# A first pair of heads prepared by a way of its own, and a new order of instructions within each pair: attention and routed experts on one core

## The chip, the cores and the metric

The kernel runs on one core of a Trainium2 chip. The metric is the device time of one launch in microseconds (us); the time of a kernel is the median of its runs. Inputs and output are float32 in the device's memory; the host only lays the inputs out anew.

The core's engines each run their own list of instructions in order: the tensor engine (PE) multiplies matrices, the vector engine (DVE), the scalar engine (ACT) and GpSimd (POOL) work elementwise or reduce, and SyncE (SP) issues most transfers (DMA). Engines wait for one another by semaphores.

## The reference

Attention over 64 heads (8 batches of 8 heads) with 1152 keys and head width 64, where two neighbouring queries are averaged first (576 queries a head), then a layer of 8 experts, to which the 4608 tokens are assigned greedily by score, at most 576 to each:

```python
# attention
q_pool = q.reshape(B, H, S // 2, 2, D).mean(axis=3)
scores = (1 / np.sqrt(D)) * np.matmul(q_pool, k.transpose(0, 1, 3, 2))
scores = scores - np.max(scores, axis=-1, keepdims=True)
attn = np.exp(scores)
attn = attn / (np.sum(attn, axis=-1, keepdims=True) + 1e-09)
out = np.matmul(attn, v)          # B=8, H=8, S=1152, D=64
# experts, on x = out as 4608 tokens of 512
logits = x @ w_gate               # 512 x 8
...
for idx in np.argsort(-logits.flatten()):      # greedy, capacity 576
    tok, e = divmod(int(idx), 8)
    if assigned[tok] < 0 and counts[e] < 576:
        assigned[tok] = e; counts[e] += 1
for e in range(8):
    out[assigned == e] = np.maximum(x[assigned == e] @ w1[e], 0) @ w2[e]   # 512 x 1024 x 512
```

## The kernel before

**Two stages.** The attention works on 32 pairs of heads, numbered 0 to 31. Then follow the assignment of tokens and the eight experts. The change lies in the attention; the code of the second stage is the same in both kernels.

**Precision.** Every number that enters a matmul is held as two 16-bit parts, high and low, whose products are added in float32. So each pair's q, k and v are split: a high part (KH, QH, the high half of V) is a scaled copy on ACT; a low part (KL, QL, the low half of V) is what the copy lost, made on DVE by one instruction that scales, subtracts and rounds (`scalar_tensor_tensor`). The scales SC and EX follow from sums of absolute values, so that the 16 bits are used well.

**The main loop.** A pair has 18 steps, two heads times nine blocks of 128 keys. In each step the PE makes scores (`qk`, L617, four matmuls of 288 columns into one of two score banks sc), ACT takes the exponential into P (L620), POOL takes P minus its upper 16 bits into PM (L623 and L624; at the steps listed in `AT["pd"]` DVE does it), and the PE multiplies P and PM with V (`av`, L634, 45 small matmuls), six steps behind the scores. At the end of a head the sums are divided out (L651 to L655). Every two pairs the gate's logits are added up (L669 to L687) and the attention's rows are stored (L749).

**The preparation of a pair** runs during the pair before it. In order: loads of q, k and v into one buffer each (QD, KD, VD: L410 to L418); q's two neighbours added (QS, L466, DVE); sums of absolute values on ACT (L427, with the scrap output VJ) and a matmul that totals them over the partitions (L431, L432); scales from the bits of the totals (VE L441, SC, EX L452 and L456); the parts QH L468, QL L470, KH L483, KL L486, V L509 and L512; copies of the parts by DMA to the layout of the score matmuls (`spread`, L493, into KA, KB, QA, QB, two buffers each). Then the row maxima of the scores, subtracted in the exponent: a block-diagonal copy of q (BD, L475, zero but for two blocks of 64 x 64) lets one matmul make the scores of both heads for 64 queries each (L535 and L545, in two banks ma and mb), and DVE reduces them (MX, L538 and L547). Nine query blocks times 1152 keys make 18 matmuls of 512 columns and some of 128. The maxima of a pair are gathered (CM, L573), transposed on the PE (L589), scaled (AU, L590), and written by DMA as an additional row of QB (L593); so the score matmul itself subtracts them.

**Pair 0** has nothing before it to hide its preparation. There BD is copied by DVE, the maxima come in 27 pieces of 384 columns (L526) into all eight PSUM banks, of which DVE reduces 18 (L530) and ACT copies nine to MS (L533), which DVE then folds (L566 to L568); one CM, one transpose (L582), and QB by DVE (L584) with the help of a diagonal mask `ndiag`, nine rows beside the 64 of a head. Before that the PE is warmed up by 50 matmuls of ones (wu, L756) and, during pair 0's maxima, by 65 more (wv, L758).

**What sets the order.** All of this is first written down as items with their reads and writes (class `Order`). For the attention the class `Cycle` then puts them in one order, from which each engine's list follows: of all items whose inputs' writers are placed, the one with the smallest number comes next. The number is looked up under the item's tag and its count within the pair, from the table TAU (from pair 1 on) or TAU0 (pair 0), plus 25 for each pair. So all pairs from 1 on have nearly the same order within, and each table entry moves an item in every pair. The tables' numbers have no meaning beyond their order. `lock` marks items that use the port which DVE and POOL share; `Cycle` doesn't read it.

## Time and profile before

| what | before |
|---|---|
| median of 3 runs | 1360.26 us (1359.87 to 1360.43) |
| the profiled execution, its device time | 1367.31 us |
| the profiled execution, span of the profile | 1365.5 us |
| PE busy | 1254.2 us, 92% |
| PE weight loads busy | 1014.6 us, 74% |
| DVE busy | 1047.8 us, 77% |
| POOL busy | 896.5 us, 66% |
| ACT busy | 806.9 us, 59% |
| mean granted PE clock | 0.968 of full speed |

Busy shares are over the whole span, in which the attention takes about the first 840 us. The page cuts the span into 40 slices and prints for each the busy tenths of an engine and the granted clock of the PE:

```profile
PE   5688899999999999999999999898999999999996
DVE  6699989899998998999999975877768768722220
POOL 2368677878788787787878872346576557568531
PEclk6899999999999999999999998999999999999998
```

One digit stands for 34.1 us. In the first two slices the PE is half busy, and its clock is granted only in part; from there to about slice 25 (the attention) PE and DVE are both near nine tenths; in the experts the PE alone is full. The heaviest groups of the attention on the engine that shares DVE's port and on ACT are:

```profile
L624 POOL TENSOR_TENSOR PM<-P 128x576 f16<-128x576 f32 x502 | 607.8, 1237 | 217.9 <-ACT P L620 109.4
L620 ACT ACTIVATE P<-sc,EX 128x576 f32<-128x576 f32 x576 | 407.1, 739 | 119.0 <-PE sc L617 113.5
```

A row names line, engine, operation, output and inputs with shapes, and the count; then the busy time and the mean ns of one; then the idle time just before these instructions and what ended most of it.

### The profile page before, as it was taken

The numbers are of one execution on the slowest core, as the hardware profiler recorded it, in microseconds if no ns is written. First come the engines' busy times: TensorE is split into PE (matmuls) and PEld (weight loads), VectorE is DVE, ScalarE is ACT, GpSimd is POOL, SyncE is SP. The second block draws the span as 40 slices with busy tenths as digits, with TensorE's granted clock in tenths as the row PEclk, the third lists the DMA queues.
The fourth block names the chain that finished last, engine by engine and source line by source line (L and its number), as shares of the span: only waits on it lengthen the run. The fifth ranks groups of instructions, "written<-read, shape, count | busy, mean of one in ns | idle before, by whom it ended". The sixth has DMA issues, their size and how long they took to land.

```text
span 1365.5 us, 38368 instructions
## 1 busy us (share of the span) xinstructions
PE 1254.2 (92%) x15456; PEld 1014.6 (74%) x15456; DVE 1047.8 (77%) x2618; ACT 806.9 (59%) x1426; POOL 896.5 (66%) x824
## 2 busy tenths in 40 slices
PE   5688899999999999999999999898999999999996
...
DVE  6699989899998998999999975877768768722220
...
POOL 2368677878788787787878872346576557568531
PEclk6899999999999999999999998999999999999998
...
GB/s 160 97 131 169 86 150 155 138 144 168 130 143 153 154 143 142 152 145 147 171 131 137 137 70 19 105 55 193 159 70 200 101 128 150 183 117 154 97 12 35
DMA packets 123534, 175.20 MB, mean 128 GB/s; under 512 B 49500, under 2 KB 86364, under 8 KB 121180
## 3 DMA queue, kind: packets, MB, share of 16 engines
...
q14 instruction: 57, 0.47, 0.1%
...
## 4 chain that ended last, share of the span: by engine, by line
PE 59%; DVE 21%; DMA 9%; issue 5%; ACT 4%; SPq 1%; POOL 0%; another core or an unknown queue 0%; DVEq 0%; POOLq 0%; ACTq 0%
PE ph L1340 13%; PE av L634 13%; PE po L1370 12%; PE sc L617 10%; DMA QA<-QH 6%; DVE MX L538 6%; DVE V L512 4%; PE mb L535 3%; PE ma L535 2%; DVE QS L466 2%; ACT VJ L427 2%; DVE QL L470 1%; DMA W<-in_w_dram,widx 1%; ACT P L620 1%; PE rt L1018 1%
## 5 line engine op out<-in xcount | busy, mean ns | idle before, releaser
L624 POOL TENSOR_TENSOR PM<-P 128x576 f16<-128x576 f32 x502 | 607.8, 1237 | 217.9 <-ACT P L620 109.4
L620 ACT ACTIVATE P<-sc,EX 128x576 f32<-128x576 f32 x576 | 407.1, 739 | 119.0 <-PE sc L617 113.5
L634 PEld LDWEIGHTS <-P 128*128 128x128 bf16 x5760 | 297.7, 98 | 32.5 <-issue 4.1
L634 PE MATMUL av<-V,P 128*128 128x65 f16 (+1 forms) x5760 | 308.8, 192 | 0.0
L634 PE MATMUL av<-V,PM 128*128 128x65 f16 x2880 | 298.6, 194 | 0.8 <-POOL PM L624 0.8
L634 PEld LDWEIGHTS <-PM 128*128 128x128 f16 x2880 | 264.6, 97 | 1.1 <-POOL PM L624 0.9
L617 PE MATMUL sc<-QA,KA 128*128 128x288 f16 x1152 | 236.8, 287 | 10.2 <-DMA QA<-QH 8.9
L617 PE MATMUL sc<-QB,KB 65*128 65x288 f16 (+1 forms) x1152 | 237.8, 287 | 0.0
L538 DVE TENSOR_REDUCE MX<-ma 128x1 f32<-128x512 f32 x279 | 191.0, 685 | 24.4 <-PE ma L535 22.9
L538 DVE TENSOR_REDUCE MX<-mb 128x1 f32<-128x512 f32 x279 | 190.8, 684 | 11.0 <-PE mb L535 10.4
L617 PEld LDWEIGHTS <-KA 128*128 128x128 f16 x1152 | 102.4, 97 | 105.5 <-issue 51.8
L1370 PE MATMUL po<-W2H,HX 128*128 128x512 f32 x512 | 164.7, 397 | 0.0
L1340 PE MATMUL ph<-XL,W1H 128*128 128x320 f32 (+1 forms) x512 | 156.2, 305 | 1.8 <-DVE XL L1273 1.3
L1340 PE MATMUL ph<-XH,W1H 128*128 128x320 f32 (+1 forms) x512 | 155.8, 304 | 0.3 <-DVE XL L1239 0.3
L1340 PE MATMUL ph<-XH,W1L 128*128 128x320 f32 (+1 forms) x512 | 155.7, 304 | 0.0
L1345 ACT ACTIVATE HX<-ph 128x320 fp32r<-128x320 f32 (+1 forms) x128 | 52.5, 411 | 148.9 <-PE ph L1340 138.8
L535 PE MATMUL mb<-KH,BD 128*128 128x512 f16 x279 | 107.8, 386 | 34.8 <-DVE MX L538 28.7
L617 PEld LDWEIGHTS <-KB 65*128 65x128 f16 (+1 forms) x1152 | 113.3, 98 | 30.5
L1370 PE MATMUL po<-W2L,HX 128*128 128x512 f32 (+1 forms) x320 | 126.7, 396 | 0.0
L535 PE MATMUL ma<-KH,BD 128*128 128x512 f16 x279 | 106.8, 383 | 7.5 <-DMA BD<-QH 6.1
L1384 POOL DMA_INDIRECT out_dram<-OT,idx x40 | 39.6, 990 | 109.0 <-ACT OT L1375 85.0
L1370 PEld LDWEIGHTS po<-W2H,HX 128*128 128x128 f32 x512 | 94.9, 188 | 17.9
...
## 6 DMA issues: line engine op xcount, KB each, us to landing
...
QA<-QH SPq DMA_DIRECT2D x128, 72.0 KB
...
```

Of the source, the lines that this page charges most:

```text
L427: od.add(t + AT["bq"] * (c == 1) + AT["bv"] * (c == 2), "ACT", dur, lambda c=c, src=src: nc.scalar.activation(VJ[:, :src.shape[1]], src, A ...
L512: od.add(t + AT["vh"] + AT["vd"] * s, "DVE", 725, lock=1, fn=lambda s=s: nc.vector.scalar_tensor_tensor(V16[i][:, s, :, 0:D], VD[0][:, s], ...
L535: od.add(t, "PE", 214, lambda: nc.tensor.matmul(m, BD[i][:, j, :], KH[i][:, 512 * c:512 * c + 512], start=True, stop=True), r=bd + [("KH", ...
L538: od.add(t, "DVE", 597, lambda: nc.vector.tensor_reduce(MX[i][:, j, c:c + 1], m, axis=AX.X, op=OP.max), r=[mk], w=[("MX", i, j, c)], tag=" ...
L617: nc.tensor.matmul(c[:, t, :288], a[i][:rows, s, ks], b[i][:rows, s, 288 * t:288 * t + 288], start=first, stop=not first)
L620: od.add(g + 0.1, "ACT", 624, lambda: nc.scalar.activation(p.rearrange("p (t q) -> p t q", t=2), c[:, :, :288], AF.Exp, scale=EX[n % 3][:, ...
L624: od.add(g + 0.2, en, dur, lock=1, fn=lambda: eng.tensor_tensor(pm, p, hi, op=OP.subtract), r=[("P32", g % NP)], w=[("PM", g % NM)], tag="pm")
L634: nc.tensor.matmul(out, w[:, qs], v, start=kb == 0 and j == 0 and y == 0, stop=kb == NKB - 1 and y == 2, skip_group_check=True)
L1340: nc.tensor.matmul(p, a[:, d, fs], b[:, d, qs], start=z == 0, stop=z == 11)
L1345: nc.scalar.activation(HH[:, f, qs], p, AF.Relu)
L1370: nc.tensor.matmul(o[:n], a[:, z, q0:q0 + n], b[:, z], start=z == 0 and y == 0, stop=z == 7, skip_group_check=True)
L1384: st = nc.gpsimd.indirect_dma_start(out=out, out_offset=bass.IndirectOffsetOnAxis(ap=idx[i][:n, c:c + 1], axis=0), in_=OT[ob][:n], in_offs ...
```

## The change

**Pair 0 by a way of its own.** The maxima are made head by head, directly from the first 64 or last 64 rows of QH and KH, so that no block-diagonal copy is needed: two heads times five query blocks (four of 128, one of 64) times three pieces of 384 keys are 30 matmuls, each reduced by DVE into MX0. Head 0 uses all eight banks, head 1 only ma and mb, while the scores of head 0 run. Each head has its own CM, transpose and two writes into QB (rows 64 to 68: five rows for 73 - 64 = nine before). ACT's copies to MS and the folds are gone. The sum of |k| is taken in two halves (VM has a fourth column, and the total another matmul). The parts are made on other engines: QH on DVE by `tensor_scalar`; k, q and v are scaled in place on ACT behind their high parts, and POOL subtracts (KL, QL, V low).

**Warm-ups.** Instead of 50 and 65 matmuls of 128 columns there are 30 and 22 of 512 columns; all may begin at once, and where each stands is a matter of the tables.

**Order.** There are three tables (pair 0, pair 1, and all later ones), and nearly all their numbers are new. The lists of steps whose PM is made on DVE become [9] for [8, 10, 11, 14] in pair 0 (`pd0`), [4, 12] for [5, 12] in pairs 1 to 30 (`pd`), and eleven steps for ten in pair 31 (`pd1`). Assumed lateness of loads (`late`) is altered too; `Cycle` doesn't read it.

The core of the diff (numbers of the tables left out but for two entries):

```diff
         def at(i):
             zero, tag, num, base = self.key[items[i][1]]
-            l = (TAU0 if zero else TAU)[tag]
+            l = (TAU, TAU0, TAU1)[zero][tag]
             return l[min(num, len(l) - 1)] + PERIOD * base
...
-       "ld": [-147.52, -112.42, -203.92], "ldv": [-55.79], "me": [-20.33, -12.03, -9.26], "mm": [-28.73, -28.43,
+       "kl": [-181.49, -190.11], "ld": [-81.78, -145.94, -308.78], "ldv": [-98.51], "me": [-20.17, -11.42, -6.47],
...
-AT = {"load": -12.4, ...
-      6, "np": 10, "nm": 10, "stick": 1, "nx": 3, "wu": 50, "pd": [5, 12], "wv": 65, "pd0": [8, 10, 11, 14], "pd1":
-      [1, 2, 4, 5, 6, 8, 10, 13, 16, 17], "d1": 2.0, "cw1": 0.7}
+AT = {"load": -14.1, ...
+      6, "np": 10, "nm": 10, "stick": 1, "nx": 3, "wu": 30, "pd": [4, 12], "wv": 22, "pd0": [9], "pd1": [0, 2, 5, 7,
+      8, 9, 10, 14, 15, 16, 17], "d1": 2.0, "cw1": 0.7}
...
+    wide = const.tile([128, 512], BF, name="wide")
+    nc.vector.memset(wide, 1.0)
...
-    VM = several(2, [128, 3], F32, "VM")
+    VM = several(2, [128, 4], F32, "VM")
-    MS = const.tile([128, NB, 384], BF, name="MS")
+    MX0 = const.tile([128, 2, 5, 3], F32, name="MX0")
...
+        if n == 0 and not a:
+            for z in range(2):
+                od.add(t, "ACT", 680, lambda z=z: nc.scalar.activation(
+                    VJ[:, :M], KD[0][:, z * M:z * M + M], AF.Abs, accum_out=VM[i][:, 3 * z:3 * z + 1]), ..., tag="abk")
...
+        if n == 0:
+            od.add(t + 1, "DVE", 640, lambda: nc.vector.tensor_scalar(QH[i], QS[0], QC, None, op0=OP.mult), lock=1, ..., tag="qh")
+            halves = [slice(z * M, z * M + M) for z in range(2)]
+            for z, h in enumerate(halves):
+                od.add(t + 1, "ACT", 665, lambda h=h: nc.scalar.activation(KH[i][:, h], KD[0][:, h], AF.Copy, scale=KS), ..., tag="kh")
+            for z, h in enumerate(halves):
+                od.add(t + 2, "ACT", 665, lambda h=h: nc.scalar.activation(KD[0][:, h], KD[0][:, h], AF.Copy, scale=KS), ..., tag="kd")
+            od.add(t + 2, "ACT", 665, lambda: nc.scalar.activation(QS[0], QS[0], AF.Copy, scale=QC), ..., tag="kd")
+            for z, h in enumerate(halves):
+                od.add(t + 3, "POOL", 1105, lambda h=h: nc.gpsimd.tensor_tensor(KL[0][:, h], KD[0][:, h], KH[i][:, h], op=OP.subtract), ..., tag="kl")
+            od.add(t + 3, "POOL", 1105, lambda: nc.gpsimd.tensor_tensor(QL[0], QS[0], QH[i], op=OP.subtract), ..., tag="ql")
+            return
...
-            if n:
-                od.add(t + 1.1, "SP", 650, bd(nc.sync.dma_start), ..., late=3500, tag="bdd")
-            else:
-                od.add(t + 1.1, "DVE", 230, lock=1, fn=bd(nc.vector.tensor_copy), ..., tag="bd")
+            od.add(t + 1.1, "SP", 650, bd(nc.sync.dma_start), ..., late=3500, tag="bdd")
...
+            if n == 0:
+                od.add(t, "ACT", 665, lambda s=s: nc.scalar.activation(V16[i][:, s, :, D:2 * D], VD[0][:, s], AF.Copy, scale=VS), ..., tag="vh")
+                od.add(t + .5, "ACT", 665, lambda s=s: nc.scalar.activation(VD[0][:, s], VD[0][:, s], AF.Copy, scale=VS), ..., tag="vd")
+                od.add(t + 1, "POOL", 1105, lambda s=s: nc.gpsimd.tensor_tensor(
+                    V16[i][:, s, :, 0:D], VD[0][:, s], V16[i][:, s, :, D:2 * D], op=OP.subtract), ..., tag="vl")
+                continue
...
         if n == 0:
-            banks = [(ma, "ma"), (mb, "mb")] + ...
+            h, j = j // 5, j % 5
+            banks = [(ma, "ma"), (mb, "mb")]
+            if not h:
+                banks += ...
             m, mk = banks[z % len(banks)]
+            r, q = slice(64 * h, 64 * h + 64), 128 if j < 4 else 64
+            od.add(t, "PE", 163, lambda: nc.tensor.matmul(
+                m[:q, :384], QH[i][r, 128 * j:128 * j + q], KH[i][r, 384 * c:384 * c + 384], start=True, stop=True), ..., tag="mm" + "01"[h])
+            od.add(t, "DVE", 463, lambda: nc.vector.tensor_reduce(MX0[:q, h, j, c:c + 1], m[:q, :384], axis=AX.X, op=OP.max), ..., tag="mr" + "01"[h])
+            return
-            if c < 2:
-                od.add(t, "DVE", 463, lambda: nc.vector.tensor_reduce(MX[i][:, j, c:c + 1], m[:, :384], axis=AX.X, op=OP.max), ..., tag="mr")
-            else:
-                od.add(t, "ACT", 371, lambda: nc.scalar.copy(MS[:, j], m[:, :384]), r=[mk], w=[("MS", j)], tag="mc")
...
-    def fold(j, t):
...
+                def both(h=h):
+                    nc.vector.tensor_reduce(CM[h][:, 64:68], MX0[:, h, :4], axis=AX.X, op=OP.max)
+                    nc.vector.tensor_reduce(CM[h][:64, 68:69], MX0[:64, h, 4], axis=AX.X, op=OP.max)
...
-    for _ in range(AT["wu"]):
-        od.add(-70, "PE", 60, lambda: nc.tensor.matmul(mb[:, :128], ones, ones, start=True, stop=True), w=["mb"], tag="wu")
-    for _ in range(AT["wv"]):
-        od.add(-42, "PE", 54, lambda: nc.tensor.matmul(av[1][:, :128], ones, ones, start=True, stop=True),
-               r=[("CM", 0, 0)], w=["av1"], first=-1, tag="wv")
+    for x in ("wu", "wv"):
+        for _ in range(AT[x]):
+            od.add(-70, "PE", 213, lambda: nc.tensor.matmul(av[1], ones, wide, start=True, stop=True), w=["av1"], tag=x)
```

What this makes of the engines' lists shows at three places. In the rows a name with a number is one buffer of a tile; L numbers are lines of the kernel they belong to.

**PE, at the end of the maxima that come ahead of the first score matmul (sc).** Before, pair 0's last maximum matmul and the transpose of its maxima, pair 1's totals of absolute values (down, floor, VM) and seven maxima matmuls of pair 1 (L535, of which the first is shown) stand ahead of the first scores:

```order
L526 MATMUL mb<-KH_83,BD_97 128x384
L582 MATMUL mb<-ident,CM_102 73x128
L431 LDWEIGHTS down
L431 MATMUL mb<-floor,down 128x4
L432 LDWEIGHTS down
L432 MATMUL mb<-VM_120,down 128x3
L535 LDWEIGHTS BD_98
L535 MATMUL ma<-KH_84,BD_98 128x512
```

After, the last of head 0's maxima matmuls, the transpose, and one matmul of head 1's maxima stand there:

```order
L564 LDWEIGHTS QH_88
L564 MATMUL av_158<-KH_85,QH_88 128x384
L618 MATMUL mb<-ident,CM_104 69x128
L564 LDWEIGHTS QH_88
L564 MATMUL mb<-KH_85,QH_88 128x384
L656 LDWEIGHTS KA_91
L656 MATMUL sc_155<-QA_95,KA_91 128x288
```

So the first scores (L656, L617 before) come behind the maxima of one head of pair 0 rather than behind those of both heads and a part of pair 1's.

**DVE, in a pair of the steady stretch.** Before, from the first piece of V's low part on (MX are maxima; ma and mb the banks; QS the sum of two neighbouring queries):

```order
L512 SCALAR_TENSOR_TENSOR V_99<-VD_117,SC_109,V_99 128x9x64
L538 TENSOR_REDUCE MX_125<-mb 128x1
L538 TENSOR_REDUCE MX_125<-ma 128x1
L470 SCALAR_TENSOR_TENSOR QL_88<-QS_118,SC_109,QH_86 128x576
L512 SCALAR_TENSOR_TENSOR V_99<-VD_117,SC_109,V_99 128x9x64
L466 TENSOR_TENSOR QS_118<-QD_116 128x576
L538 TENSOR_REDUCE MX_125<-mb 128x1
```

After, in the same place:

```order
L550 SCALAR_TENSOR_TENSOR V_101<-VD_119,SC_111,V_101 128x9x64
L576 TENSOR_REDUCE MX_127<-mb 128x1
L576 TENSOR_REDUCE MX_127<-ma 128x1
L550 SCALAR_TENSOR_TENSOR V_101<-VD_119,SC_111,V_101 128x9x64
L576 TENSOR_REDUCE MX_127<-mb 128x1
L480 TENSOR_TENSOR QS_120<-QD_118 128x576
L576 TENSOR_REDUCE MX_127<-ma 128x1
```

The group QL, V, QS is taken apart: a maximum stands between V and QS, and QL has left. Where it went shows behind the scale EX of the same pair. Before:

```order
L456 TENSOR_SCALAR EX_112<-mb,EX_112 128x1
L538 TENSOR_REDUCE MX_126<-ma 128x1
L547 TENSOR_REDUCE MX_126<-mb 128x4
L624 TENSOR_TENSOR PM_142<-P_132 128x576
L486 SCALAR_TENSOR_TENSOR KL_85<-KD_115,SC_109,KH_83 128x576
L624 TENSOR_TENSOR PM_139<-P_129 128x576
L486 SCALAR_TENSOR_TENSOR KL_85<-KD_115,SC_109,KH_83 128x576
L547 TENSOR_REDUCE MX_126<-ma 128x1
```

After:

```order
L470 TENSOR_SCALAR EX_114<-mb,EX_114 128x1
L663 TENSOR_TENSOR PM_143<-P_133 128x576
L585 TENSOR_REDUCE MX_128<-mb 128x4
L576 TENSOR_REDUCE MX_128<-ma 128x1
L502 SCALAR_TENSOR_TENSOR QL_90<-QS_120,SC_111,QH_88 128x576
L663 TENSOR_TENSOR PM_141<-P_131 128x576
L515 SCALAR_TENSOR_TENSOR KL_87<-KD_117,SC_111,KH_85 128x576 x2
L576 TENSOR_REDUCE MX_128<-mb 128x1
L585 TENSOR_REDUCE MX_128<-ma 128x1
```

One PM has moved up to stand right behind EX, and QL, the other PM and both halves of KL form one group of four.

**SP, in a pair of the steady stretch**, from the two transfers that write the row of maxima into QB (AU) on; L410, L414 and L418 before are the loads of q, k and v, the rest copies of parts. Before:

```order
L593 DMA QB_95<-AU 1x9x64 x2
L493 DMA KB_92<-KH_84 64x1152
L493 DMA QB_96<-QL_88 64x576
L418 DMA VD_117<-in_v_dram 128x1152
L493 DMA KA_90<-KL_85 64x1152
L493 DMA QB_96<-QL_88 64x576
L410 DMA QD_116<-in_qt_dram 128x1152
L493 DMA QA_93<-QH_86 64x576
```

After:

```order
L632 DMA QB_97<-AU 1x9x64 x2
L522 DMA QA_95<-QH_88 64x576
L426 DMA VD_119<-in_v_dram 128x1152
L522 DMA KA_92<-KL_87 64x1152
L522 DMA QA_96<-QH_89 64x576
L522 DMA KB_94<-KH_86 64x1152
L522 DMA QB_98<-QL_90 64x576
L522 DMA KA_92<-KH_86 64x1152
L418 DMA QD_118<-in_qt_dram 128x1152
```

The copy of q's high part into the buffer of the pair that runs (QA_93 before, QA_95 after) stood behind both loads and now stands ahead of them; the copies for the next pair (QA_96) are spread over the pair.

133 lines of the change are left out of this document (74 added, 59 removed), and 55 rows, old and new, of tables (TAU, TAU0, TAU1).

## The prediction

> **What bounds the kernel now.** I read the page's header and chain, then the line of the scale factor EX (one per pair, so its starts are the clock of the attention), then stretches of one pair each, then who waits for whom. The steady stretch is pairs 5 to 31, from 147.10 to 782.60.
>
> ```profile
> span 1365.5 us, 38368 instructions
> PE 59%; DVE 21%; DMA 9%; issue 5%; ACT 4%; SPq 1%; POOL 0%; another core or an unknown queue 0%; DVEq 0%; POOLq 0%; ACTq 0%
> L452 ACT ACTIVATE EX<-SC x32: 294/297/298, 12.7 to 782.6; 128x1 f32<-128x1 f32 x32
> 64.10:88.70 24.60, 20.62 (x313) 15.48 (x309) 21.50 (x37) 16.99 (x29) 14.06 (x13) 0.93 0.51 131
> 196.40:221.02 24.62, 22.54 (x380) 18.01 (x377) 23.20 (x42) 19.74 (x34) 19.40 (x17) 1.00 0.48 119
> 221.02:245.55 24.53, 23.38 (x391) 18.21 (x388) 21.96 (x43) 20.04 (x35) 19.34 (x17) 1.00 0.71 174
> 466.20:490.00 23.80, 23.55 (x394) 18.46 (x390) 22.16 (x44) 20.01 (x35) 18.59 (x16) 1.00 0.74 179
> 147.10:782.60 635.50, 598.79 (x9880) 472.00 (x9877) 589.64 (x1087) 517.48 (x871) 503.98 (x416) 1.00 0.58 146
> ```
>
> The profiled execution took 1367.31 us, 0.52% over the median 1360.26; I sum against 1367.31 and multiply by 1360.26/1367.31 = 0.9948 at the end. The chain that ended last lies 59% on the PE and 21% on DVE over all stages. A steady pair takes (782.6 - 147.1)/26 = 24.44 us. PE is busy 598.79/26 = 23.03 of it, DVE 589.64/26 = 22.68: no engine is full, yet both are near it, so the period is set by waits between them. Pairs differ: 24.62 where the PE is busy 22.54 (no gate work), 24.53 or 23.80 where it is busy 23.4 to 23.5 (gate work). In the 23.80 one the PE hardly rests, and that is how far a pair can fall. Who makes the PE wait in these 26 pairs, and what DVE stands on:
>
> ```profile
> PE mb L535 <- DVE MX L538: 18.0, 13, 1.4
> PE sc L617 <- DMA QA<-QH: 8.9, 12, 1.3
> L538 DVE TENSOR_REDUCE MX<-ma 128x1 f32<-128x512 f32 x235 | 160.9, 684 | 17.8 <-PE ma L535 16.6
> L512 DVE SCALAR_TENSOR_TENSOR V<-VD,SC,V 128x576 f16<-128x576 f32 x52 | 54.2, 1042 | 0.0
> L466 DVE TENSOR_TENSOR QS<-QD 128x576 f32<-128x576 f32 x26 | 31.8, 1222 | 0.0
> L441 DVE TENSOR_SCALAR VE<-mb 128x3 int32<-128x3 int32 x26 | 4.2, 162 | 11.3 <-PE mb L432 11.2
> ```
>
> The first row is 13 waits of 1.4 us, one in every second pair. This is what stands behind them:
>
> ```profile
> 207.87 0.80 DVE L470 SCALAR_TENSOR_TENSOR QL<-QS,SC,QH 128x576 f16<-128x576 f32 x1
> 208.59 1.70 DVE L512 SCALAR_TENSOR_TENSOR V<-VD,SC,V 128x576 f16<-128x576 f32 x1
> 210.22 1.70 DVE L466 TENSOR_TENSOR QS<-QD 128x576 f32<-128x576 f32 x1
> 211.84 0.68 DVE L538 TENSOR_REDUCE MX<-mb 128x1 f32<-128x512 f32 x1
> 223.59 0.75 DVE L624 TENSOR_TENSOR PM<-P 128x576 f16<-128x576 f32 x1
> 224.26 0.81 DVE L486 SCALAR_TENSOR_TENSOR KL<-KD,SC,KH 128x576 f16<-128x576 f32 x1
> 226.38 0.28 DVE L547 TENSOR_REDUCE MX<-ma 128x1 f32<-128x128 f32 x1
> 118.82 2.25 POOL L624 TENSOR_TENSOR PM<-P 128x576 f16<-128x576 f32 x2 [3.17 <-issue]
> ```
>
> QL, V and QS run one behind another; V and QS take 1.70 where QL takes 0.80, and POOL's PM runs between. The two engines shut each other out there: DVE makes no maximum from 207.87 to 211.84, and the PE, with two banks for maxima, stands. Four locked operations in 223.59 to 226.38 without such a wait take 2.79, 0.70 each; a PM alone needs 1.10 (the second of the two in 2.25, the first being 1.15 long).
>
> **The start.** The order of the first 64 us:
>
> ```profile
> 1.83 4.83 PE L756 MATMUL mb<-ones 128*128 128x128 bf16 x50 [1.83 <-DVE floor L337]
> 29.18 2.50 PE av L758 x22
> 55.43 0.22 PE ma L535
> 11.36 0.16 PE L432 MATMUL mb<-VM,down 128*128 128x2 bf16 x1 [4.70 <-ACT VJ L427]
> 2.71 1.36 DVE L397 TENSOR_SCALAR ndiag<-scratch 128x576 f32<-128x576 int32 x1
> 17.73 0.56 DVE L530 TENSOR_REDUCE MX<-av 128x1 f32<-128x384 f32 x1 [0.66 <-PE av L526]
> 19.00 0.56 DVE L530 TENSOR_REDUCE MX<-av 128x1 f32<-128x384 f32 x1
> 19.48 0.55 DVE L530 TENSOR_REDUCE MX<-sc 128x1 f32<-128x384 f32 x1
> 35.94 0.18 DVE L573 TENSOR_REDUCE CM<-MX 128x9 f32<-128x27 f32 x1
> 37.29 0.81 DVE L584 SCALAR_TENSOR_TENSOR QB<-mb,CB,ndiag 9x576 f16<-9x576 f32 x1
> 38.38 0.16 DVE L441 TENSOR_SCALAR VE<-mb 128x3 int32<-128x3 int32 x1 [0.29 <-PE mb L432]
> 43.22 0.60 PE ma L535
> 43.84 0.70 DVE MX L538
> 48.46 0.97 PE sc L617 x4
> 63.49 0.18 DVE CM L573
> 64.10 0.30 ACT L452 ACTIVATE EX<-SC 128x1 f32<-128x1 f32 x1
> 73.68 1.37 ACT L620 ACTIVATE P<-sc,EX 128x576 f32<-128x576 f32 x2 [4.21 <-PE sc L617]
> ```
>
> Scales at 11.4 us, first maximum 17.73, pair 0's maxima closed at 35.94, pair 1's scales at 38.38, its maxima from 43.84 to 63.49, and the first scores only at 48.46, since seven maxima matmuls of pair 1 stand ahead of them. Pair 2's EX at 64.10 is where the steady rhythm begins, and DVE's queue leads to it: what brings that EX forward moves all that follows.
>
> **The change, step by step: the start.** (1) To the first maximum. 33 long warm-ups now stand ahead of the scale matmul. At the slow clock 128 columns take 2.50/22 = 0.11, so 512 take 0.45; at full clock 0.22 (row of 55.43). The 50 short ones took 4.83 where 50 x 0.11 is 5.5 and 50 x 0.055 is 2.75: some 34 were slow, 3.8 us. So nine long ones slow, 24 fast: 2.0 + 4.0 + 5.3 = 11.3, and the earlier K and q loads bring nothing (11.36 before). Were all slow, it would be 16.9; the slow clock lasting 3.8 us is the nearer row. The clock rule of the Trainium skill, "TensorE: Matmul & The Clock Gate", Part 1, is that about 4 us of steady work lift a halved clock, and the trace agrees with its 3.8; by the rule the sum stays, and by a clock that never lifted the start would lose 5.6. Then SC, which no longer queues behind the |v| sum on ACT; on DVE ndiag (between half and the whole of the 1.36 in its row, where POOL's memsets ran beside it) and QH (no such row; the 0.81 of K low at 224.26, same size with two inputs, is the upper bound, half of it the lower): ready at 13 to 14, first maximum about 13.7, four earlier. I take the lower ones, as POOL is still then.
>
> (2) Head 0 has 15 reductions at 0.48 (19.00 to 19.48) = 7.2, with 0.5 of small ones between: closed at 21.6. Transpose and QB took 37.29 + 0.81 - 35.94 = 2.2 before and take less with half the columns: first scores about 23.5 for 48.46. The 25 us are not won, as DVE still owes the rest. K's and q's low parts are made on POOL meanwhile, three at a PM's 1.1 or so (there is no row for them): done by 18, so their copies to the score tiles have 5 us to land; should they take longer, the first scores wait and DVE goes on with head 1.
>
> (3) Head 1: 15 x 0.48 = 7.2, pair 1's QS 0.7, transpose and QB again 2: pair 1's scales near 34 for 38.38. The copies on ACT that went cost nothing, ACT having waited there; the folds on DVE are in what 17.73 to 35.94 took.
>
> (4) Pair 1's own preparation: on ACT stand QH, K high, both V, |q| of pair 2 and the other K high, six at 0.69 (1.37 for two at 73.68) and 1.2 of small ones, 5.4 in all, ahead of its first maximum, 40.1 for 43.84. DVE's six locked operations (4.2 at 0.70) fit under it, as POOL has only nine PMs from 24 on (10 us) and then nothing. Then twenty maxima without a break at 0.60 (211.84 less one maximum on either side) = 12, since the new PE order has no scores between them; before, the same twenty took 63.49 - 43.84 = 19.65, with V, QL, QS, PM and the waits of a slow PE between. EX of pair 2: 34 + 5.4 + 0.7 (matmul) + 12 + 0.6 (scales, as 63.49 to 64.10) and some 0.8 of hand-overs = 53.5 for 64.10, **10.6 earlier**. Cover: K and V of pair 2 are reloaded at about 42, behind K low of pair 1, and needed at 53, so 5 us of slack; their |.| sums stand on ACT ahead of pair 0's second half, so seven of its 18 exponentials come behind that EX, 4.8 us, and POOL rests from 35 to 47. Before, ACT waited 4.21 in that place (73.68), so about 0.6 is lost: I take **-10**; 6 if the reloads are late, 13 if pair 1 begins without the ACT chain.
>
> **The steady pairs** (29 from 64.10 on, at 24.44). Counts are the same: two PMs, QL, two K, two V and QS locked on DVE, 16 PMs on POOL. Moved: QL goes from between the two V to the K group, each V and QS stands alone between maxima, a PM fills the place behind EX, one exponential stands between the |v| sum and SC, and q's second-head copies are issued ahead of the VD and QD loads. The PE's waits on MX (18.0) and QA (8.9) are the ones attacked, 26.9 in 26 pairs. By the PE's side, half of it coming back as other waits: 13. By DVE's side: stalls in V and QS were 52 x 0.23 + 26 x 0.47 = 24.2, 0.93 a pair in three entries (0.31 each). Clean, DVE works 22.68 - 0.93 = 21.75; idle now 1.77, of which the 16.6 us before MX (0.64 a pair) are filled by PM, and of the 11.3 before VE (0.43) half go: 0.9 stays. Five entries at 0.31 give 1.55: 24.2, a gain of 0.24 x 29 = 7. Between the two I take **-10** (24.1). Bounds: at best 30, since 16 PMs and eight locked operations shut each other out for 16 x 1.10 + 8 x 0.72 = 23.4; at worst +31 (below).
>
> **At nothing:** the tables' block stands on DVE in one piece between two maxima as before, and I allow it 1 either way; one PM more on DVE in the last pair, where the PE is full:
>
> ```profile
> 800.00:825.00 25.00, 24.74 (x415) 19.99 (x412) 14.98 (x28) 16.58 (x25) 18.79 (x17) 1.00 0.19 50
> ```
>
> The cover there is the PE itself; without it a PM costs 0.75. Pair 0's three PMs moved to POOL lie in its rest. The experts are untouched.
>
> Sum: 1367.31 - 10 - 10 = 1347.3, times 0.9948: **1340**.
>
> **Rivals.** *Only the start* (chance 0.14): the new waits eat the steady gain; for it, DVE's and PE's loads stay the same; against it, the two waits attacked recur pair by pair; 1357.3, or 1350. *To the floor* (0.12): every pair at 23.4, as the 23.80 one nearly is: 1367.3 - 10 - 30, or 1320. *Slower* (0.12): three locked entries become five, and POOL is busy 16 x 1.10 = 17.6 of the 18.6 us that DVE's own eight leave. If each entry waits for half a PM, 0.57, DVE needs 21.75 + 0.9 + 2.85 = 25.5: 29 x 1.06 = +31 - 10 = +21, or 1381. It decides from 21.75 + 0.9 + 5w = 24.44 + 10/29, that is w = 0.43; against it 0.31 now, QS alone having 0.47. The rule in the Trainium skill's "SBUF — State Buffer", Who interferes with whom, speaks for this rival: the port pair is an exclusive lock, and who issues first keeps it for the whole instruction. The 1.70 of V and QS agree. *No change* (0.05): the lead at pair 2 is lost again on pair 0's late exponentials and PMs, and the pairs stay at 24.4: 1360.
>
> **The numbers.** My forecast, 1328 to 1349, has 0.57. Faster 0.57 + 0.14 + 0.12 = 0.83, same (within 0.2%, 2.7 us, about what a measurement can tell) 0.05, slower 0.12. The range: at the low end most of the floor case with the start at 13, at the high end start-only with the start at 6 and a little more: 1318 to 1358; slower and no-change stay outside, 0.17.
>
> **What would show it.** The first score matmul at 23 to 24 us; EX of pair 2 at 52 to 57; the waits of PE on MX and on QA in the steady pairs gone from 18.0 and 8.9 to under 10 together; V's mean under 1042 ns and QS's under 1222; the last EX near 763. Wrong would be: EX of pair 2 at 60 or later (steps 3 and 4), or pairs at 24.5 and more with V, QS, QL and PM at 1.2 us and more (the lock).

## The result and the profile after

The changed kernel takes 1330.48 us, the median of four runs (1328.04 to 1331.98), against 1360.17 before: a ratio of 0.978 with a 95% interval of 0.9763 to 0.9797, 29.7 us or 2.2% faster. The forecast was 1340, so 20 us faster. The time lies in the range, and the sign was right; the two terms of 10 us each were both wrong, in opposite directions.

The profiled execution took 1328.04 us, 39.3 less than that of before (1367.31). Of these, 33.5 us are there at the start of the last EX (749.1 after, 782.6 before), and 5.9 lie behind it: 577.0 us from that point to the end of the span, 582.9 before. That stretch holds the last pair's steps and the experts. The twelve kernels below took 575.6 to 581.4 us there, and e2_old_pairs and e6_ungroup, which have the old order in the last pair, took 575.6 and 577.4. So the long tail most likely belongs to the one execution of before, whose device time was 7 us over its median; there is no second trace of it that could show this.

First the header, the chain of work that ended last and the line of EX on the page of the profile after (EX: shortest, mean and longest in ns, then the first and last start in us):

```profile
span 1326.1 us, 38213 instructions
PE 74%; DVE 19%; issue 3%; ACT 1%; DMA 1%; POOL 1%; POOLq 0%; DVEq 0%; ACTq 0%
L466 ACT ACTIVATE EX<-SC x32: 280/294/297, 15.0 to 749.1; 128x1 f32<-128x1 f32 x32
```

PE's share of the chain went from 59% to 74%, DMA's from 9% to 1%: the kernel now waits for the PE's own work.

The steady pairs, from the windows view (start:end, length, then busy time of PE, PEld, DVE, ACT and POOL, granted clock, DMA share, GB/s): a pair with gate work, and pairs 5 to 31.

```profile
213.20:236.70 23.50, 23.50 (x386) 18.29 (x385) 22.44 (x43) 20.00 (x34) 19.54 (x17) 1.00 0.68 172
143.80:749.10 605.30, 600.63 (x9878) 472.99 (x9877) 580.85 (x1087) 515.21 (x872) 507.92 (x417) 1.00 0.59 154
```

A pair takes 605.30/26 = 23.28 us for 24.44, and PE is busy 600.63/26 = 23.10 of it, practically the 23.03 of before. What went is the PE's rest: 635.50 - 598.79 = 36.7 us in 26 pairs before, 605.30 - 600.63 = 4.7 now. In the single pair there is none at all. Who makes the PE wait there (the waits view, us in total, times, longest), with the groups of DVE in the same stretch (busy us, mean ns | idle us ahead of them):

```profile
PE ma L573 <- DVE MX L576: 2.8, 13, 0.2
L550 DVE SCALAR_TENSOR_TENSOR V<-VD,SC,V 128x576 f16<-128x576 f32 x52 | 45.1, 868 | 0.0
L480 DVE TENSOR_TENSOR QS<-QD 128x576 f32<-128x576 f32 x26 | 28.5, 1096 | 0.0
L663 DVE TENSOR_TENSOR PM<-P 128x576 f16<-128x576 f32 x52 | 46.8, 899 | 0.1
L455 DVE TENSOR_SCALAR VE<-mb 128x3 int32<-128x3 int32 x26 | 4.2, 161 | 0.8
```

The waits on MX (18.0) and QA (8.9) that the change attacks are down to 2.8 and nothing. V and QS are shorter than before (868 for 1042 ns, 1096 for 1222), but PM on DVE is longer (899; 0.75 us in the row of 223.59 before). PM now fills the place behind EX, where DVE used to wait for a maximum's matmul (timeline of DVE: start, us; the first row is before, the others after):

```profile
197.72 0.69 DVE L538 TENSOR_REDUCE MX<-ma 128x1 f32<-128x512 f32 x1 [0.64 <-PE ma L535]
190.60 0.22 DVE L470 TENSOR_SCALAR EX<-mb,EX 128x1 f32<-128x1 f32 x1
190.74 1.13 DVE L663 TENSOR_TENSOR PM<-P 128x576 f16<-128x576 f32 x1
```

The idle time ahead of VE fell from 11.3 us to 0.8. With it went a third wait of the PE, one that the prediction did not price: ahead of the totals which VE needs, the PE waited for ACT's sums of absolute values (before, in the stretch 147.1 to 782.6; the list of after has no such row).

```profile
PE mb L432 <- ACT VJ L427: 4.8, 14, 0.4
```

The start did not go as forecast. The rows of the timeline that answer to the steps:

```profile
22.05 0.17 DVE L604 TENSOR_REDUCE CM<-MX 128x4 f32<-128x12 f32 x1
24.00 0.42 PE L656 MATMUL sc<-QA,KA 128*128 128x288 f16 x2
24.11 0.56 DVE L567 TENSOR_REDUCE MX<-mb 128x1 f32<-128x384 f32 x1 [0.41 <-PE mb L564]
40.06 0.14 DVE L604 TENSOR_REDUCE CM<-MX 128x4 f32<-128x12 f32 x1
43.17 0.16 DVE L455 TENSOR_SCALAR VE<-mb 128x3 int32<-128x3 int32 x1 [0.29 <-PE mb L447]
49.12 0.68 DVE L576 TENSOR_REDUCE MX<-ma 128x1 f32<-128x512 f32 x1
59.38 1.16 ACT L439 ACTIVATE VJ<-KD 128x1152 bf16<-128x1152 f32 x1 [11.02 <-DMA KD<-in_kt_dram]
64.18 0.69 DVE L576 TENSOR_REDUCE MX<-mb 128x1 f32<-128x512 f32 x1 [1.47 <-PE mb L573]
65.59 0.29 ACT L466 ACTIVATE EX<-SC 128x1 f32<-128x1 f32 x1
```

Up to the first scores at 24.00 all comes when it should, and they are 24.5 us earlier than before (48.46). Then head 1's fifteen reductions take from 24.11 to 40.06, 16 us where I had 7.2, and EX of pair 2 starts at 65.59, 1.5 us *later* than before. The windows of that time show why (same columns; the granted clock is third from the end):

```profile
16.00:24.00 8.00, 5.08 (x23) 1.66 (x22) 6.24 (x16) 3.68 (x7) 4.68 (x6) 1.00 0.78 202
24.00:26.00 2.00, 1.35 (x8) 0.51 (x7) 1.11 (x2) 0.74 (x1) 0.90 (x2) 0.92 0.83 242
26.00:42.00 16.00, 15.90 (x89) 7.25 (x89) 7.39 (x16) 8.81 (x14) 9.71 (x9) 0.50 0.21 74
65.00:70.00 5.00, 5.00 (x81) 4.64 (x81) 3.39 (x7) 4.62 (x9) 2.41 (x3) 0.50 0.27 48
70.00:72.00 2.00, 2.00 (x43) 1.79 (x40) 0.91 (x3) 0.88 (x3) 0.72 (x2) 0.98 0.93 283
```

From 16 to 24 the PE has little to do (5.08 of 8 us), at 24 to 26 the clock begins to fall (0.92), and from 26 on it is 0.50, through the whole of head 1 and pair 1's preparation, up to 70 us. DVE meanwhile is busy 7.39 of 16 us: it waits for the halved PE.

### The profile page after: what moved, and what is told of

Same layout as the page of the kernel before. It is cut to its first block, busy times and chain, and to the rows that moved or that the text cites. A ratio compares the mean times of both kernels' runs of the same rounds, so it can differ in the third digit from the quotient of the medians.

```text
span 1326.1 us, 38213 instructions
## 1 busy us (share of the span) xinstructions
PE 1264.2 (95%) x15398; PEld 1008.8 (76%) x15398; DVE 1035.6 (78%) x2619; ACT 803.7 (61%) x1423; POOL 907.0 (68%) x831
## 4 chain that ended last, share of the span: by engine, by line
PE 74%; DVE 19%; issue 3%; ACT 1%; DMA 1%; POOL 1%; POOLq 0%; DVEq 0%; ACTq 0%
PE sc L656 17%; PE ph L1374 15%; PE av L673 14%; PE po L1404 13%; DVE MX L576 5%; PE ma L573 4%; PE mb L573 4%; DVE KL L515 2%; DVE PM L663 1%; PE av L708 1%; PE rt L1052 1%; DVE MX L585 1%; DVE ST L1170 1%; PE av L796 1%; PE av L720 1%
## 5 line engine op out<-in xcount | busy, mean ns | idle before, releaser
L673 PEld LDWEIGHTS <-P 128*128 128x128 bf16 x5760 | 299.9, 98 | 31.9 <-issue 1.6
L656 PE MATMUL sc<-QB,KB 65*128 65x288 f16 (+1 forms) x1152 | 239.4, 289 | 0.0
L656 PE MATMUL sc<-QA,KA 128*128 128x288 f16 x1152 | 238.2, 288 | 1.2 <-ACT P L659 1.2
L656 PEld LDWEIGHTS <-KA 128*128 128x128 f16 x1152 | 104.3, 97 | 80.3 <-issue 33.5
L656 PEld LDWEIGHTS <-KB 65*128 65x128 f16 (+1 forms) x1152 | 113.9, 99 | 31.1
```

What stands on the lines that cost most here:

```text
L656: nc.tensor.matmul(c[:, t, :288], a[i][:rows, s, ks], b[i][:rows, s, 288 * t:288 * t + 288], start=first, stop=not first)
L673: nc.tensor.matmul(out, w[:, qs], v, start=kb == 0 and j == 0 and y == 0, stop=kb == NKB - 1 and y == 2, skip_group_check=True)
```

## The experiments

The questions were: which part of the change brings the gain, the start or the pairs; which of the moves within a pair; and what the start loses to. Times are medians, each with its ratio to the kernel before, run beside it on the same chip, and the 95% interval; "pairs" is the mean length of pairs 5 to 31 from the starts of EX in the profile (24.44 before, 23.28 after), "EX of pair 2" its start (64.1 and 65.6), "EX of pair 31" the last one (782.6 and 749.1).

### Start or pairs

**e1_new_pairs.** Before, with the changed table and places of PM from pair 2 on (TAUN is the TAU of after):

```diff
-            l = (TAU0 if zero else TAU)[tag]
+            l = (TAU0 if zero else TAUN if base >= 2 else TAU)[tag]
```

> The kernel before with the new order (and the new list of steps whose PM is on DVE) from pair 2 on; the first two pairs as before. If the gain is the steady order's, as the trace of the changed kernel reads (EX of pair 2 at 65.6 us there for 64.1, then 23.28 us a pair for 24.44): the PE's waits on MX and QA vanish, the pairs fall to 23.3, and the time comes to 1327 to 1333. If start and pairs share it half and half, as the prediction had it: 1348 to 1352.

**e2_old_pairs.** The reverse: after, with before's table and places of PM from pair 2 on (TAUP is the TAU of before).

```diff
-            l = (TAU, TAU0, TAU1)[zero][tag]
+            l = (TAUP if base >= 2 else TAU, TAU0, TAU1)[zero][tag]
```

> The changed kernel with the old order and the old list from pair 2 on; the new start of pairs 0 and 1. If the new start is worth nothing: 1356 to 1364, EX of pair 2 near 65. If it is worth the 10 us of the prediction: 1350. Pairs at 24.4 by both.

**e5_old_start.** Before, with the whole of the changed TAU, so pair 1 too runs by it, and the changed places of PM in all pairs but the first. Only the preparation and run of pair 0 and the tables TAU0 are those of before.

```diff
-"pd": [5, 12], ... "pd1": [1, 2, 4, 5, 6, 8, 10, 13, 16, 17]
+"pd": [4, 12], ... "pd1": [0, 2, 5, 7, 8, 9, 10, 14, 15, 16, 17]
```

> The kernel before with the new table and the new lists for all pairs from 1 on (so without the change of order between pairs 1 and 2 of the run with the new pairs); only pair 0's own preparation is the old one. If the new start is worth nothing of its own and the loss of that run lay at the seam: pairs 2 and 3 at 23 us, and the time of the changed kernel, 1328 to 1333. If the new start is worth the 6 us between them: 1334 to 1340.

| kernel | median us | ratio | EX of pair 2 | EX of pair 5 | EX of pair 31 | pairs |
|---|---|---|---|---|---|---|
| after | 1330.48 | 0.978 (0.9763 to 0.9797) | 65.6 | 143.8 | 749.1 | 23.28 |
| e1_new_pairs | 1336.83 | 0.9824 (0.9803 to 0.9845) | 66.3 | 154.0 | 759.3 | 23.28 |
| e2_old_pairs | 1373.85 | 1.0099 (1.0077 to 1.0121) | 67.1 | 159.2 | 794.4 | 24.43 |
| e5_old_start | 1330.33 | 0.9775 (0.9751 to 0.98) | 66.3 | 147.1 | 752.4 | 23.28 |

The length of a pair follows its table to 0.01 us, whatever start it has: 23.28 three times with the new one, 24.44 and 24.43 with the old one. e5_old_start has the time of after without its start, so **the new start is worth nothing that the medians can tell** (the two ratios differ by 0.0005, and their intervals are 0.003 to 0.005 wide), at most the 3.3 us by which its last EX is later in the profile (they arise between pairs 2 and 5; EX of pair 2 is 0.7 later). e1 and e2 show a price that nothing in the prediction had: where two tables meet, pairs 2 to 4 run badly. e1 differs from e5 only in where the new table begins and loses 154.0 - 147.1 = 6.9 us there; e2 reaches pair 5 12.1 us later than before, of which 1.5 are the new start's own (65.6 for 64.1). This is why e1 and e2 lie outside what was expected of them. So "e2 is slower than before" says nothing against the new start; the means of the steady pairs are the fair comparison.

### Which move within a pair

The visible moves were put back into the new order one at a time, and put into the old order one at a time.

**e3_group, e8_qs_only, e10_ql_only.** After, with QL back between the two pieces of V, QS back right behind V, or both, from pair 2 on (the numbers are places in the new table; e8 has the qs alone, e10 the ql alone):

```diff
-            l = (TAU, TAU0, TAU1)[zero][tag]
+            l = (dict(TAU, ql=[-22.45], qs=[-47.37]) if base >= 2 else TAU, TAU0, TAU1)[zero][tag]
```

> The changed kernel with QL moved back between the two halves of V, and QS right behind, from pair 2 on. If this group of locked operations was what made the PE wait for maxima: V and QS at 1.7 us in every second pair again, a wait of 1 us or more of the PE on MX there, 14 x 1.0 to 1.4 = 14 to 20 us slower than the changed kernel, 1344 to 1350. If the other moves did it: within 3 us of the changed kernel.

> The changed kernel with QS right behind the second half of V from pair 2 on, QL left where the change put it. If it is two locked operations in a row that cost (the PE's two banks for maxima run out): half or more of the 51 us that QL, V and QS together cost, 1350 to 1380. If three are needed: within 5 us of the changed kernel.

> The changed kernel with QL back between the two halves of V from pair 2 on, QS left behind a maximum. QS alone right behind V cost 9 us, and QL and QS together 51. If the two costs add: 36 to 46 us slower than the changed kernel, 1366 to 1377. If it needs the three in a row: 5 to 20 us slower, 1335 to 1350.

| put back | median us | ratio | pairs | PE idle in 26 pairs |
|---|---|---|---|---|
| nothing (after) | 1330.48 | 0.978 (0.9763 to 0.9797) | 23.28 | 4.7 |
| QS | 1339.53 | 0.9848 (0.9819 to 0.9877) | 23.60 | 8.6 |
| QL | 1353.4 | 0.9939 (0.9922 to 0.9955) | 24.07 | 19.2 |
| both | 1381.28 | 1.0139 (1.0115 to 1.0164) | 25.13 | 36.8 |

QS costs 9.0, QL 22.9, both 50.8, more than the 31.9 of their sum, and none of the three lies where it was expected. In e3_group these waits and groups answer:

```profile
PE mb L573 <- DVE MX L576: 24.0, 13, 1.9
L550 DVE SCALAR_TENSOR_TENSOR V<-VD,SC,V 128x576 f16<-128x576 f32 x52 | 56.4, 1084 | 0.0
L480 DVE TENSOR_TENSOR QS<-QD 128x576 f32<-128x576 f32 x26 | 31.7, 1218 | 0.0
```

V and QS are back at the lengths they had before (1084, 1218), and with them the PE's wait for MX: 13 times, 1.9 us at the longest, in every second pair. The mechanism that the prediction read from before (three locked operations in a row on DVE, no maximum, two banks full) is confirmed, in the kernel after.

But the waits are not all of the 51 us. Pairs 5 to 31 of e3_group are 48.1 us longer than those of after; the PE's rest makes 32.1 of it, and 16.0 is time in which the PE is busy (616.6 us for 600.6). In this stretch the clock falls:

```profile
152.50:805.90 653.40, 616.62 (x9878) 480.70 (x9877) 594.17 (x1087) 516.19 (x872) 521.26 (x417) 0.98 0.56 142
```

It goes to 0.50 eight times, each time for 3.4 us and within 4 us after the start of one of the thirteen waits of 1.9 us; by an estimate that costs up to 8 x 3.4 / 2 = 13.6 us. In after, e8_qs_only and e10_ql_only the clock in pairs 5 to 31 is 1.00. So the long wait costs a second time, in the clock, and this may be a part of what both moves cost beyond their sum. How large a part is not shown, as the PE's busy time grew in e8_qs_only and e10_ql_only too (by 4.4 and 6.1 us).

**e6_ungroup and e9_three_moves.** The same move made alone in the kernel before: QL into the K group, QS two maxima behind V; e9 also takes the first PM out of the K group, to a place one maximum behind EX.

```diff
-"ql": [-22.62], "qs": [-47]
+"ql": [-73.56], "qs": [-46.6]
...
-"pd": [5, 12]
+"pd": [4, 12]
```

> The kernel before with two numbers changed: QL goes to the group of K's low parts, and QS stands one or two maxima behind V; nothing else of the order. If that group alone made the steady loss, as the run with the group put back says: V and QS at 0.75 to 1.2 us, no wait of the PE on MX, pairs at 23.3 to 23.7, 1330 to 1342. If the other moves are needed as well (a PM behind EX, the copies of q): pairs at 24.2 or more, 1352 to 1365.

> The kernel before with QL in K's group, QS two maxima behind V, and step 4 in place of step 5 as the first whose PM is on DVE, which takes one PM out of K's group: four locked operations there (QL, KL, PM, KL), as in the changed kernel, for five in the run with QL and QS moved alone. If what cost there was the fifth one, which pushed the last maxima, CM and the transpose back: no KL of 1.7 us ahead of CM, pairs at 23.3 to 23.8 us, 1330 to 1343. If the rest of the new order is needed: pairs at 24.2 or more, 1352 or more.

e6_ungroup takes 1370.68 (ratio 1.0071, 1.0045 to 1.0096; pairs 24.78), e9_three_moves 1426.83 (1.0473, 1.0454 to 1.0493; pairs 26.68). Both miss: what costs 51 us to put back brings nothing alone, but loses. In e6_ungroup, the wait of the PE, the end of the K group on DVE (which runs from 199.61 with PM, QL, KL, PM, KL) and CM:

```profile
PE mb L589 <- DVE CM L573: 11.4, 13, 0.9
202.40 1.70 DVE L486 SCALAR_TENSOR_TENSOR KL<-KD,SC,KH 128x576 f16<-128x576 f32 x1
...
204.93 0.18 DVE L573 TENSOR_REDUCE CM<-MX 128x9 f32<-128x27 f32 x1
```

V is clean now (803 ns in its group, 1042 before), and the wait for MX behind it is gone. But the lock has moved with QL: the K group is longer by one operation, its last KL takes 1.70, and CM, the gathering of the maxima, comes late, 7.4 us behind EX (197.55 to 204.93) for 5.8 in before (196.87 to 202.64). The PE's list still has the transpose that needs CM in its old place, so the PE stands there instead. With the PM moved too, that wait comes in every pair, and a second one beside it:

```profile
PE mb L589 <- DVE CM L573: 26.7, 26, 1.5
PE mb L535 <- DVE MX L547: 21.4, 26, 1.1
```

In the changed kernel the K group (QL, PM, KL, KL from 192.99 to 195.85) meets no such wait, and CM comes 6.2 us behind EX (190.60 to 196.76). POOL's rows tell a difference; the first is e6_ungroup, the second after (in brackets how long POOL stood still before):

```profile
202.13 5.18 POOL L624 TENSOR_TENSOR PM<-P 128x576 f16<-128x576 f32 x4 [2.79 <-issue]
195.52 4.72 POOL L663 TENSOR_TENSOR PM<-P 128x576 f16<-128x576 f32 x4 [2.65 <-PE av L673]
```

POOL stands still from 192.87 to 195.52, which covers nearly the whole group of after; in e6_ungroup it begins again at 202.13, ahead of the last KL. In e9_three_moves it begins again at 210.82, ahead of the last PM and the last KL, which both take 1.70 (at 210.91 and 212.54), and CM comes 8.8 us behind EX. Nor does e9_three_moves have the whole DVE order of after: there PM stands right behind EX, here a maximum stands between them; there the group is QL, PM, KL, KL, here QL, KL, PM, KL; there QS stands one maximum behind V, here two. So these moves alone do not bring the gain, and **only the whole new table was seen to bring it**. Whether it needs the rest of DVE's order or the new places of PE, ACT, SP and POOL was not taken apart.

**e4_qa_late.** After, with one of the two copies of q's high part into QA put back behind the loads of VD and QD on SP:

```diff
-            l = (TAU, TAU0, TAU1)[zero][tag]
+            l = (dict(TAU, spr=TAU["spr"][:9] + [4.44, -0.36] + TAU["spr"][11:]) if base >= 2 else TAU, TAU0, TAU1)[zero][tag]
```

> The changed kernel with one of q's second-head copies back behind the loads of VD and QD, from pair 2 on. If the place behind the loads was what made the score matmuls wait for QA: waits of 0.7 to 1.3 us in half of the pairs or more, 8 to 20 us slower, 1339 to 1350. If that wait came from the late QH and not from the queue: within 3 us of the changed kernel.

1329.0 us (ratio 0.9768, 0.9748 to 0.9788; pairs 23.36): no effect on the time, and one wait of 0.2 us for QA in the steady pairs. And in e2_old_pairs, where the old order runs behind the new start, the PE's wait for QA is 5.3 us where it was 8.9, while the one for MX is 17.9 for 18.0 and the pairs are as long as before:

```profile
PE mb L593 <- DVE MX L596: 17.9, 13, 1.4
PE sc L676 <- DMA QA<-QH: 5.3, 6, 1.4
```

So of the two waits attacked, it is the one on MX that goes with the pair's length; the one on QA can shrink or its cause return without any change of it.

### What the start loses to

**e7_hot.** After, with nine matmuls of ones (512 columns each, into the bank av[0], which is free then; nothing reads them): five ahead of the transpose of head 0's maxima, four behind it.

```diff
+HOT = [((1, 'augt', 0, 0), True, 5), ((1, 'augt', 0, 0), False, 4)]
...
+    for _ in range(sum(x[2] for x in HOT)):
+        od.add(-70, "PE", 213, lambda: nc.tensor.matmul(av[0], ones, wide, start=True, stop=True), w=["av0"], tag="wx")
```

> The changed kernel with nine more matmuls of ones, five ahead of the transpose of head 0's maxima and four behind it, where the PE idles for 1.2 and 1.0 us. If the granted clock falls at 25.7 us for those gaps and the slow clock makes the 17 us of head 1's maxima: clock 1.00 in 26 to 40, the second transpose at 33 to 35 us for 41.4, EX of pair 2 at 57 to 60 for 65.6, 4 to 8 us faster than the changed kernel, 1322 to 1327. If the PE's stops between the scores bring it down anyway: EX of pair 2 at 64 or later and within 2 us of the changed kernel.

1321.21 us (ratio 0.9709, 0.9684 to 0.9733), 9.3 less than after, and **the best version**, together with e12_hot_pair1, which can't be told from it. The windows and the rows of the timeline that changed:

```profile
16.00:24.00 8.00, 7.30 (x33) 2.46 (x31) 6.51 (x18) 4.11 (x7) 4.67 (x6) 1.00 0.84 204
26.00:36.00 10.00, 9.47 (x90) 5.18 (x90) 7.52 (x16) 8.43 (x14) 8.67 (x8) 1.00 0.38 132
36.00:42.00 6.00, 1.25 (x10) 0.88 (x10) 4.66 (x10) 4.66 (x10) 1.48 (x2) 0.85 0.29 51
34.85 0.15 DVE L611 TENSOR_REDUCE CM<-MX 128x4 f32<-128x12 f32 x1
36.95 0.16 DVE L462 TENSOR_SCALAR VE<-mb 128x3 int32<-128x3 int32 x1 [0.29 <-PE mb L454]
58.68 0.29 ACT L473 ACTIVATE EX<-SC 128x1 f32<-128x1 f32 x1
```

With PE busy 7.30 of 8 us ahead of the first scores, the clock stays at 1.00 to 36 us. Head 1 is closed at 34.85 for 40.06, pair 1's scales come at 36.95 for 43.17, EX of pair 2 at 58.68 for 65.59, and the last EX at 742.7 for 749.1: what is won by 37 us is still there at 743. (The traces differ by 7.7 us in the whole; that of after is of the fastest of its runs.) The clock falls again in 36 to 42, where the PE is idle between head 1 and pair 1's first maximum (busy 1.25 of 6), so two more kernels went for that.

**e12_hot_pair1.** e7_hot, with 14 more such matmuls behind pair 1's totals and one behind each of its 18 maxima matmuls of 512 columns (into av[1]).

```diff
+HOT = [((1, 'augt', 0, 0), True, 5), ((1, 'augt', 0, 0), False, 4), ((2, 'vs', 0, 1), False, 14), ((2, 'mm', 0, 1), False, 1), ... ((2, 'mm', 17, 1), False, 1)]
```

> The run with nine more matmuls of ones, and besides 14 more behind the totals of pair 1 and one behind each of pair 1's 18 maxima matmuls; no work of the kernel moved. If the slow clock from 40 to 60 still costs there: clock 1.00 in that stretch, pair 1's twenty maxima at 0.60 apart for 0.68 (1.6 us), and the matmuls behind them at twice the speed (1 to 2 us): EX of pair 2 at 56 to 57.5 for 58.7, 2 to 4 us faster than the run with nine, 1317 to 1319.5. If DVE alone paces that stretch: within 1.5 us of the run with nine, 1320 to 1323.

Ratio 0.9702 (0.9679 to 0.9725; 1325.77 against 1365.31 of before beside it), not told apart from e7_hot's 0.9709, so the 2 to 4 us that were hoped for did not come. The clock was 1.00 to 56 us, and still EX of pair 2 came at 59.70, 1.0 later than in e7_hot:

```profile
53.49 1.16 ACT L446 ACTIVATE VJ<-KD 128x1152 bf16<-128x1152 f32 x1 [11.72 <-DMA KD<-in_kt_dram]
58.29 0.69 DVE L583 TENSOR_REDUCE MX<-mb 128x1 f32<-128x512 f32 x1 [3.75 <-PE mb L580]
```

ACT waits 11.72 us for the reload of K (KD) of pair 2, which its sum of absolute values needs; the exponentials of pair 0 stand behind that sum, scores on the PE behind them, and the last maximum behind the scores (3.75 us). From |K| to EX of pair 2 it is 6.2 us in all three kernels: 59.38 to 65.59, 52.46 to 58.68, 53.49 to 59.70. The load took 8.8 us from its issue to this use (44.72 to 53.49), 7.4 in e7_hot (45.09 to 52.46); why is not shown. So behind pair 1's scales it is this load that sets the time, and not the clock.

**e11_fill.** e7_hot, with the same 14 matmuls, and with useful work instead of more ones: pair 0's steps of av and its later scores stand between pair 1's maxima, and pair 2's sums of |k| and |v| later on ACT.

```diff
+            if zero == 2 and tag == "mm":
+                return 16 + 0.7 * num
...
+                if tag[:2] == "av" and 3 <= g < 12:
+                    return 16.3 + 1.4 * (g - 3) + 0.7 * (tag[2] == "1")
...
+            if zero == 0 and base == 2 and tag == "abs" and num != 1:
+                return 26 + num / 2
```

> The run with nine more matmuls of ones, and besides: 14 more behind the totals of pair 1, and pair 0's steps 3 to 11 of P times V and its scores from step 12 on set between pair 1's maxima matmuls, where the PE stood for most of 16 us at the slow clock while it waited for DVE. If the time is set by the PE's work left at the start of pair 2: the clock stays at 1.00 from 42 to 60, the work of some nine steps is out of the way, EX of pair 2 at 55 to 60 with shorter pairs behind it, 4 to 8 us faster than the run with nine, 1313 to 1317. If DVE's queue sets it and the filling delays the maxima as much as it saves: 1319 to 1324.

1332.54 us (ratio 0.9791, 0.9774 to 0.9807), 11.3 worse than e7_hot and worse than either case expected. The work of pair 0 that is done early leaves the PE without any later (PE is the second number behind the length):

```profile
60.00:64.00 4.00, 1.40 (x31) 0.93 (x27) 2.54 (x8) 2.22 (x6) 0.00 (x0) 1.00 0.00 0
64.00:68.00 4.00, 0.63 (x2) 0.17 (x2) 3.49 (x7) 1.79 (x3) 0.00 (x0) 0.60 0.58 105
```

EX of pair 2 is at 62.0, later than in e7_hot, then the PE has 2.0 us of work in 60 to 68 and the clock halves after all. DVE, busy 3.49 of 4 at that time, has the maxima still to make. By these rows, early scores help only as far as DVE's queue moves with them.

## Why the prediction was right in sum and wrong in its terms

**Where it failed: step (3) of the start, "15 x 0.48 = 7.2".** It took DVE's pace from 19.00 to 19.48, where the PE ran at full clock ahead of it, for a stretch in which the PE sets the pace. Measured are 16.0 us, 8.8 more. e7_hot divides them: with the clock kept at 1.00, head 1 takes from 24.53 to 34.85, 10.3 us. So 5.6 us are the halved clock. Of the other 3.1, pair 1's QS on DVE takes 0.76, which the sum had as a term of its own; the rest I put down to pair 0's scores and av, which stand between the maxima in the PE's list and which I had left out (in e7_hot the PE is busy 9.55 us of 24.50 to 34.90). I had weighed the clock for the warm-ups only (step 1) and not for the gap that the change opens behind them, 16 to 24 us.

| point | forecast | measured |
|---|---|---|
| totals on the PE | 11.3 | 10.96 |
| first maximum | 13.7 | 12.83 |
| head 0 closed | 21.6 | 22.05 |
| first scores | 23.5 | 24.00 |
| pair 1's scales | 34 | 43.17 |
| first maximum of pair 1 | 40.1 | 49.12 |
| EX of pair 2 | 53.5 | 65.59 |

Steps (1) and (2) hold to within a microsecond. From the scales to the first maximum of pair 1 it is 5.9 us, forecast 6.1.

**Step (4): "5 us of slack" for the reloads.** There was none: pair 1's maxima lasted from 49.12 to 64.87, 15.7 us for the 12 forecast, and e12_hot_pair1 shows that with a fast PE it is no better, as K of pair 2 comes too late. Its load was issued at 51.32, 8.1 us behind pair 1's scales, as forecast (42 for 34), and came to use 8.1 us later, at 59.38. What I had wrong is when it is needed: not with EX ("needed at 53") but 6.2 us ahead of it. I had named the case ("6 if the reloads are late") and given it little weight. Steps (3) and (4) make 9.2 + 3.7 of the 12.1 us by which EX of pair 2 is late; the end was 0.8 shorter than forecast. **The start's -10 measured +1.5 at EX of pair 2, and nothing that can be told in the whole** (e5_old_start).

**The steady pairs: right mechanism, too small a term.** The -10 measured 35: from EX of pair 2 to that of pair 31 it was 718.5 us and is 683.5. 30.2 of it lie in pairs 5 to 31, 4.8 in pairs 2 to 4. My two ways of working it out gave 13 and 7 since both took for granted that something comes back: by the PE's side half of its 26.9 us of waits as other waits, by DVE's side 0.31 us of stall for each of five entries into the lock. Hardly anything did. Of the 26.9 us of waits 24.1 went, and the PE's rest fell by 32.0 in all, as the wait for ACT's sums (4.8 us) went too. And the stalls turned out not to be the measure: beyond the clean lengths I used (V 0.81, QS and PM 0.75) they are 52 x 0.06 + 26 x 0.35 + 52 x 0.15 = 20 us now, 24.2 before. They have hardly shrunk. They are spread, with a maximum between one and the next, so that the PE's two banks never fill up, and PM uses time in which DVE had to wait anyway. Stalls that stand apart cost the PE 2.8 us in 26 pairs, and three operations in a row cost it 18.0, 1.4 at a time.

**The sum was right in part by luck.** The start came 11.5 us worse than its term, the pairs 25 us better, and the two errors have opposite signs. By an estimate from these, the start as forecast would have given about 1319 with the pairs as measured, and the pairs as forecast about 1355 with the start as measured; both lie outside 1328 to 1349.

**At nothing.** The tables' block and the PMs at the ends gave no sign of a cost: the stretch behind the last EX is as long as in all the other kernels.

**The rivals.** *Only the start* is the opposite of what happened: e5_old_start has the gain without the start, e2_old_pairs the start without a gain. *To the floor* describes the pairs (23.28, I had 23.4), and in sum it misses by the start only; its reason was another one, though. It took POOL and DVE shutting each other out as the floor, while it is the PE that is full, 23.10 of 23.28. *Slower* needed five entries at 0.43 us and more; they cost 20/26 = 0.77 a pair, 0.15 each. The rule of the Trainium skill that stood beside it ("SBUF — State Buffer", Who interferes with whom: an exclusive lock, held for the whole instruction) agrees with the 1.70 of the last KL in e6_ungroup, ahead of which POOL had begun its PM; what decides here, though, is who waits behind the one that is held up. *No change* fell with the pairs.

**What would show it**: the first scores, the waits on MX and QA, V and QS came as written; EX of pair 2 "at 60 or later" was named as the sign against steps (3) and (4), and it is the sign that came; the last EX near 763 came at 749.

## What to carry to other kernels

Before you price a stretch at one engine's pace, ask at which clock its feeder runs there: a start that is made quicker by leaving the PE idle can pay for it with a halved clock, and nine cheap matmuls (1.25 + 1.03 us in the trace) were worth 9.3 by the medians. A locked or slow operation costs what it makes the bound engine wait, not its own length: put something that frees the bound engine's buffers between one and the next. And a move is worth what the order around it makes of it: moves of the kind that cost 51 us to take back lost 10 when they were made alone in the old order, and two good tables joined in the middle lost 7 to 11.

## What the runs showed of the chip

**The halved clock can last through busy time.** In 26 to 42 us the PE is busy 15.90 of 16.00, for 16 us, at a clock of 0.50 throughout. It rose some 5 us after a dense run of small av matmuls began at 64.98 (0.98 in 70 to 72), and in the kernel before some 4 us after that of the warm-ups at 29.18 (0.50 in 29 to 33, 0.98 in 33 to 35). The rule of the Trainium skill that step (1) weighed ("TensorE: Matmul & The Clock Gate", Part 1: about 4 us of steady work lift a halved clock) agrees with these two and not with 26 to 42. The number of columns makes it plausible that the PE was busy there without being dense: the busy time of a matmul is modelled, and the matmuls that the trace has in 26 to 42 stand in groups like these (x and the count, busy us, mean ns | idle; as many score matmuls come from QB and KB, two more groups of 15 av, and 11 maxima matmuls in all).

```profile
L656 PE MATMUL sc<-QA,KA 128*128 128x288 f16 x16 | 5.3, 436 | 0.0
L673 PE MATMUL av<-V,PM 128*128 128x65 f16 x15 | 2.6, 244 | 0.0
L564 PE MATMUL mb<-KH,QH 64*128 64x384 f16 x5 | 2.5, 504 | 0.0
```

Together these are 32 x 288 + 45 x 65 + 11 x 384, some 16,400 columns. At the 2.50/22 us for 128 that a dense run took at this clock, an estimate of 14.6 us, so over 1 us of the 16 is short stops. In 65 to 70 the same estimate (75 av of 65 columns, four scores of 288) gives 5.4 for 5.00 us, so no stop at all. The Trainium skill, "TensorE: Matmul & The Clock Gate", A second HAM failure mode: psum-queue depth-cycling, tells of such a case, short rests between groups of matmuls that keep the clock from staying up; the short rests agree with it, but here the clock did not go up and down, it stayed at 0.50 from 25.7 to 70 us, and no run tried the case. That the maxima of head 1 use only 64 rows is another possible reason why it did not rise; they do not bring it down by themselves, since in e7_hot the same matmuls ran at 1.00 from 26 to 36.

**The clock fell without one long gap.** In 16 to 24 the PE had 2.9 us of rest in 8, the two longest 1.2 and 1.0 us; by the 0.92 of 24 to 26 the clock was halved at about 25.7. With the PE busy 7.30 of 8 in that stretch (e7_hot) it stayed. In the steady pairs single waits did it too: in e3_group eight of thirteen waits of 1.9 us were followed by 3.4 us at 0.50, while the thirteen of 1.4 us in before left the clock of pairs 5 to 31 at 1.00. Why eight and not all thirteen is not shown.

One number of the description above is to be corrected: a step's av is 15 matmuls (five query blocks times three), not 45.
